# A seventh pass of the sequence DFT as seven block products, with two block sums made by accumulating DMAs

## The chip, the cores and the metric

The kernel runs on one core of a Trainium2 chip. The metric is the device time of one launch in microseconds (us); lower is better. A difference of 0.2% (1.4 us) is about what the measurement of this kernel can tell from no change.

## The reference

The reference is one block of an FNet: a Fourier mixing layer and then a gated feed-forward layer, both on a pre-normalized input with a residual. S = 2048 rows, D = 448 columns, Df = 1792.

```python
def _A_ref(x, dft_seq_re, dft_seq_im, dft_hid_re, dft_hid_im):
    a = jnp.einsum("bsd,ed->bse", x, dft_hid_re)
    b = jnp.einsum("bsd,ed->bse", x, dft_hid_im)
    y = jnp.einsum("ts,bse->bte", dft_seq_re, a) - jnp.einsum("ts,bse->bte", dft_seq_im, b)
    return y
def _B_ref(x, w_gate, w_up, w_down):
    g = jnp.einsum("bsd,df->bsf", x, w_gate)
    u = jnp.einsum("bsd,df->bsf", x, w_up)
    h = _gelu(g) * u
    return jnp.einsum("bsf,fd->bsd", h, w_down)
x = A_x
h = x + _A_ref(_layernorm(x), A_dft_seq_re, A_dft_seq_im, A_dft_hid_re, A_dft_hid_im)
h2 = h + _B_ref(_layernorm(h), B_w_gate, B_w_up, B_w_down)
```

## The kernel before

The kernel computes in f32 accuracy with f16 operands: each f32 operand is split into a high f16 part (`hi_part`, L108, on ScalarE/ACT) and a low f16 remainder (`lo_part`, L112 and L114, on VectorE/DVE), and each product is three f16 matmuls (hi·hi, hi·lo, lo·hi). There are three stages on TensorE (PE):

1. The DFT along the sequence (L637 and L509). The matrix W comes from DRAM in pieces, one piece per step, and every four steps make one pass. There are `N_STEPS` = 64 steps: 16 for the first two output pairs, and then twelve passes of four steps.
2. The DFT along the hidden dimension (`hid_mm`, L719), which is laid between the passes: 21 matmuls `y` for each half of an output pair.
3. The feed-forward, with gate/up products (L1028) in three blocks of 14 rounds `t`, and the down products (L1232) beside the last two blocks.

The order of all work is written out by hand: the program is issued in one loop over the steps `n`, and the tables `DFT_F`, `JIT_F`, `early`, `after`, `turns` and `PREP_AT` say in which step or round a piece stands. Each engine runs its own instructions in that order. SyncE (SP) issues all DMAs of the kernel before, also in that order.

A pass is computed in one of two ways. A *direct* pass (steps below `FAST`) has 24 matmuls of 448 columns a step. A *fast* pass (steps from `FAST` = 40 on, which are the last six passes) takes each pair of input rows and output rows as a 2x2 block product with seven block products instead of eight (Strassen-Winograd): 2 x 7 products x 3 terms = 42 matmuls of 224 columns a step, into four PSUM banks `acc_f`. It needs four sums of W's blocks, named S1 to S4 (`fast_sums`, L460 to L462, DVE), besides the raw blocks, and four sums of the rows of x, named T1 to T4 (`t_load`, `t_norm`, `t_sums`, `t_hi`, `t_lo`), which are made once in earlier steps. At the end of a pass `fast_out` combines the seven results on DVE (L538) and splits them into `zs`, and `z_turn` transposes `zs` by four DMAs.

The W data of one step are called a *unit* here. Units are prepared two or more steps ahead (`fast_at`): `seq_load` (SP, into `wr`), `fast_sums` (DVE), `fast_raw` (ACT hi, DVE lo of three raw blocks), `fast_split` (ACT hi, DVE lo of the four sums). The tiles `wr` and `sums` share a ring of five slots (tag `wr`): a load into a slot waits on SP until the DVE work that reads the slot's former tile is done.

The gate/up weights come in 14 chunks `f`. For each, `Weights` loads the raw data (SP), makes sums (DVE), splits them (ACT and DVE), and stores the f16 result in DRAM for the later blocks. Nine chunks (`DFT_F`) are split beside the DFT, the other five (`JIT_F` = 4, 6, 8, 10, 12) in the first feed-forward block, in round `t` = f - 2. GpSimd (POOL) computes nothing in the DFT; in the feed-forward it forms sums of the down weights (`down_sums`) and products (L1122).

Of the kernel before, what the change touches and what calls it, by code (L numbers as in the profile page):

```python
# [9 lines left out]
F32 = mybir.dt.float32  # L10
AF = mybir.ActivationFunctionType
ALU = mybir.AluOpType

P = 128
# [12 lines left out]
D_SC = 64.0  # L27
# [5 lines left out]
def kernel(  # L33
# [73 lines left out]
    def hi_part(dst, src, scale=1.0):  # L107
        A.activation(dst, src, AF.Copy, scale=scale)  # L108

    def lo_part(dst, src, hi, scale=1.0):  # L110
        if isinstance(scale, float) and scale == 1.0:
            V.tensor_sub(dst, src, hi)  # L112
        else:
            V.scalar_tensor_tensor(dst, src, scale, hi, op0=ALU.mult, op1=ALU.subtract)  # L114
# [293 lines left out]
    def step_of(n):  # L408

        k, qq = divmod(n - NT, 4)  # L410
        return 2 + k // 2, k % 2, qq

    def seq_load(n):
        wr[n] = dft.tile([P, 8 * P], F32, tag="wr", bufs=5, name=f"wr{n}")
        if n < NT:
            nc.sync.dma_start(wr[n].rearrange("p (b t) -> p b t", b=4), w_seq[8 * (n % 2) + n // 2])
            return
        p, part, qq = step_of(n)
        for i in range(2):
            dst = wr[n][:, i * 4 * P : (i + 1) * 4 * P].rearrange("p (g t) -> p g t", g=2)  # L420
            nc.sync.dma_start(dst, w_seq[8 * p + 2 * qq + i][:, 2 * part : 2 * part + 2, :])
# [24 lines left out]
    fast_w, fast_s, fast_t, fast_acc, fast_e = {}, {}, {}, {}, {}  # L446

    def fast_views(n):
        raw = wr[n].rearrange("p (i b t) -> p i b t", i=2, b=4)
        s = fast_s[n].rearrange("p (s i t) -> p s i t", s=4, i=2)  # L450
        src = raw[:, :, 0:3].rearrange("p i b t -> p i (b t)")
        dst = fast_w[n][0][:, :, : 6 * P].rearrange("p l (i b) -> p l i b", i=2)
        return raw, s, src, dst

    def fast_sums(n):
        fast_s[n] = dft.tile([P, 8 * P], F32, tag="wr", bufs=5, name=f"sums{n}")
        fast_w[n] = [fast_tile(n, k, **place) for k, place in enumerate(fast_places(n))]
        raw, s, src, dst = fast_views(n)
        by_block = raw.rearrange("p i b t -> p b i t")
        V.tensor_add(s[:, 0:2], by_block[:, 1:3], by_block[:, 3:4].to_broadcast([P, 2, 2, P]))  # L460
        V.tensor_add(s[:, 2], s[:, 1], raw[:, :, 1])
        V.tensor_add(s[:, 3], raw[:, :, 0], s[:, 2])  # L462
# [7 lines left out]

    def fast_raw(n):

        raw, s, src, dst = fast_views(n)
        hi_part(dst[:, 0], src, D_SC)
        lo_part(dst[:, 1], src, dst[:, 0], D_SC)

    def fast_split(n):

        w = fast_w[n][1]
        for part in slice(0, 4 * P), slice(4 * P, 8 * P):  # L480
            hi_part(w[:, 0, part], fast_s[n][:, part], D_SC)
        lo_part(w[:, 1], fast_s[n], w[:, 0], D_SC)

    def fast_a(n, i, l, name):
        if name in FORMS:
            k = 2 * FORMS.index(name) + i
# [247 lines left out]


    gu, gw = {}, {}
    DFT_F = ((13, 16, 0), (11, 18, 1), (9, 20, 0), (7, 22, 1), (5, 25, 0), (3, 27, 1), (0, 29, 0), (1, 33, 0), (2, 37, 0))
    JIT_F = range(4, 13, 2)

    early, after = {}, {}  # L740

    def at(where, n, *what):
        where.setdefault(n, []).extend(what)
# [49 lines left out]
    for j, n in ((0, 17), (1, 20), (4, 24), (5, 28), (6, 31), (2, 35), (3, 38), (7, 41)):  # L793
# [42 lines left out]
    for n in range(N_STEPS):  # L836
# [89 lines left out]
        for half in range(2):  # L926
# [3 lines left out]
                    z_out(*key)  # L930
            for what in after.get((n, half), ()):
                what()
    gu[JIT_F[0]] = Weights(JIT_F[0], JIT_F[0] % 3)
    z_turn(NP - 1)
    down_sums(0)
    gu[JIT_F[1]] = Weights(JIT_F[1], JIT_F[1] % 3)
# [331 lines left out]
    for q, t0, step, when in ((2, 5, 3, AT_A), (3, 14, 6, AT_B)):  # L1268
# [22 lines left out]
    right.close()  # L1291
    ps_ff = {
        tag: ctx.enter_context(tc.tile_pool(name=f"ps_{tag}", bufs=1, space=bass.MemoryType.PSUM, reuse_waits="tile"))
        for tag in ("a3", "X", "Y", "Z", "a0", "a1", "a2")
    }
    ps_ff["tr"] = ps_tr

# [7 lines left out]
    cur.x1()  # L1305
    cur.z1()
    prev = None
    PREP_AT = {0: 0, 1: 1, 3: 2, 5: 3, 7: 4, 9: 5, 11: 6}
    for t in range(NF):
        w = gu.get(t + 2) if t + 2 in JIT_F else None  # L1310
        n = PREP_AT.get(t)
# [46 lines left out]
        if t == 0:  # L1358
            down_sums(1)
        if t == NF - 1:  # L1360
            dn_lo(0)
        cur.z1()
# [209 lines left out]
```

## Time and profile before

| | |
|---|---|
| median of 3 runs | 703.41 us (703.22 to 703.43) |
| the profiled execution | 703.2 us |
| its span, first to last instruction | 701.1 us |
| PE busy in the span | 696.3 us |
| DVE, ACT, POOL busy | 551.0, 400.0, 95.4 us |
| mean granted TensorE clock | 1.000 |

The profile is of one execution. Its busy times say how long an engine had an instruction in it; a busy PE is not PE at its peak, so the time of a group of matmuls is read from the chain of work that ended last, which gives when a run of matmuls began and how long it carried the chain. `PEld` is the load of the stationary operand, which overlaps with PE. `SPq` is SP's queue of DMA issues; "to landing" is the time from a DMA's issue to its data being there. DMA share is the mean busy share of the 16 DMA engines; it is a sum of packet times, and it can pass 100%.

### The profile page before, as it was taken

What the parts mean: (1) busy time and instruction counts of PE and PEld (TensorE: products, weight loads), DVE (VectorE), ACT (ScalarE), POOL (GpSimd) and SP (SyncE); (2) the same over time, 40 slices, a digit from 0 to 9 for tenths busy, and PEclk for the clock granted to TensorE, in tenths of its full rate; (3) what the DMA queues carried; (4) which work ended last, traced back from release to release, by engine and by line L of the source; (5) the groups of instructions that cost most, each with busy time, mean ns of one, the idle gap of its engine ahead of it and who ended that gap; (6) DMA issues with size and microseconds to landing.
All of it is one profiled execution on the core that took longest, in us unless ns stands there. A gap on an engine that the chain in (4) does not pass through costs nothing.

```text
span 701.1 us, 13638 instructions
## 1 busy us (share of the span) xinstructions
PE 696.3 (99%) x5164; PEld 500.6 (71%) x5164; DVE 551.0 (79%) x1187; ACT 400.0 (57%) x787; POOL 95.4 (14%) x88
## 2 busy tenths in 40 slices
PE   9999999999999999999999999999999999999998
PEld 5555555555557889997644444469999999999997
DVE  7998667786798999986547798767777867899786
ACT  5876556666676566564526666555555453655631
POOL 0000000000000000000223333311020111232224
PEclk9999999999999999999999999999999999999999
DMA  8798578999997487384836878797879985877612
GB/s 276 252 255 303 121 267 227 334 288 289 269 287 195 141 195 200 117 205 179 233 125 212 288 242 236 189 326 231 245 209 326 247 299 170 318 274 276 239 39 79
DMA packets 116321, 161.29 MB, mean 230 GB/s; under 512 B 61984, under 2 KB 80544, under 8 KB 116256
## 3 DMA queue, kind: packets, MB, share of 16 engines
q1 hardware_dynamic: 116256, 160.43, 76.0%
q8 instruction: 40, 0.66, 0.4%
q14 instruction: 25, 0.20, 0.1%
HBM read 112.16 MB, written 34.34 MB: 209 GB/s over the span
## 4 chain that ended last, share of the span: by engine, by line
PE 98%; issue 1%; DMA 0%; DVE 0%; ACT 0%
PE acc L637 26%; PE acc_d L1232 15%; PE pY L1028 15%; PE acc_f L509 14%; PE pZ L1028 10%; PE pX L1028 10%; PE y L719 9%; DMA x<-in_x_dram 0%; ACT dn_w L108 0%; ACT v L958 0%; DVE st_x L122 0%; DVE xs L149 0%; DVE hr L1508 0%; ACT sd_x L129 0%; DVE r_x L373 0%
## 5 line engine op out<-in xcount | busy, mean ns | idle before, releaser
L637 PE MATMUL acc<-xs,ws 128*128 128x448 f16 x960 | 183.1, 352 | 0.1
L1028 PEld LDWEIGHTS <-gw 128*128 128x128 f16 x1443 | 140.9, 98 | 51.6
L637 PEld LDWEIGHTS <-ws 128*128 128x128 f16 x960 | 93.9, 98 | 87.7 <-DVE ws L114 0.2
L1232 PE MATMUL acc_d<-wd,dn_w 128*128 128x224 f16 x1008 | 110.6, 259 | 0.0
L1232 PEld LDWEIGHTS <-dn_w 128*128 128x128 f16 x1008 | 97.0, 98 | 1.9
L1028 PE MATMUL pY<-hops,gw 128*128 128x256 f16 (+1 forms) x629 | 98.1, 298 | 0.0
L509 PEld LDWEIGHTS <-ws 128*128 128x128 f16 x1008 | 96.6, 98 | 1.3
L1122 POOL TENSOR_TENSOR hs<-hs,c 128x256 f32<-128x256 f32 (+1 forms) x42 | 59.5, 1417 | 247.6 <-ACT c L1120 185.3
L114 DVE SCALAR_TENSOR_TENSOR ws<-wr,ws 128x1024 f16<-128x1024 f32 (+2 forms) x66 | 72.0, 1092 | 20.8 <-ACT ws L108 16.3
L108 ACT ACTIVATE ws<-wr 128x1024 f16<-128x1024 f32 (+2 forms) x66 | 61.9, 941 | 13.4 <-DMA wr<-in_w_seq_dram 8.0
L509 PE MATMUL acc_f<-t,ws 128*128 128x224 f16 x576 | 68.2, 259 | 0.0
L1028 PE MATMUL pZ<-hops,gw 128*128 128x256 f16 (+1 forms) x407 | 67.1, 298 | 0.0
L1028 PE MATMUL pX<-hops,gw 128*128 128x256 f16 (+1 forms) x407 | 67.1, 298 | 0.0
L719 PE MATMUL y<-wh,z 128*128 128x448 f16 x336 | 66.2, 352 | 0.0
L1073 ACT ACTIVATE pY<-pX 128x256 f32<-128x256 f32 (+1 forms) x42 | 18.4, 439 | 66.3 <-PE pX L1028 63.0
L215 POOL TENSOR_TENSOR wd_s<-wd 128x448 f32<-128x448 f32 x7 | 9.7, 1390 | 337.1 <-DVE e L538 336.3
L509 PE MATMUL acc_f<-xs,ws 128*128 128x224 f16 x432 | 55.1, 259 | 0.0
L719 PEld LDWEIGHTS <-z 128*128 128x128 f16 x336 | 32.9, 98 | 29.7
L1038 DVE SCALAR_TENSOR_TENSOR c<-pZ,u 128x256 f32<-128x256 f32 (+1 forms) x42 | 21.4, 510 | 38.8 <-PE pZ L1028 22.8
L1084 ACT ACTIVATE u<-pY 128x256 f32<-128x256 f32 (+1 forms) x42 | 19.1, 454 | 53.5 <-PE pY L1028 53.4
L112 DVE TENSOR_TENSOR dn_w<-dn_s,dn_w 128x640 f16<-128x640 f32 x48 | 41.5, 865 | 1.5 <-ACT dn_w L108 1.4
L108 ACT ACTIVATE dn_w<-dn_s 128x640 f16<-128x640 f32 x48 | 34.9, 728 | 12.1 <-DVE dn_s L1194 12.0
(144 smaller groups left out, 909.5 us busy)
## 6 DMA issues: line engine op xcount, KB each, us to landing
gw<-w_dram SPq DMA_DIRECT2D x37, 896.0 KB, 6.5
wr<-in_w_seq_dram SPq DMA_DIRECT2D x100, 256.0 KB, 4.6
hid_dram<-hs SPq DMA_DIRECT2D x27, 512.0 KB, 5.9
hid<-hid_dram SPq DMA_DIRECT2D x54, 256.0 KB, 5.8
w_dram<-gu_w SPq DMA_DIRECT2D x14, 896.0 KB, 6.5
gu_raw<-in_w_gu_dram SPq DMA_DIRECT2D x28, 384.0 KB, 6.1
wr<-in_w_seq_dram SPq DMA_DIRECT2D x14, 512.0 KB, 5.2
x<-in_x_dram SPq DMA_DIRECT2D x16, 224.0 KB, 3.1
```

Source lines behind the costliest of these rows:

```text
L108: A.activation(dst, src, AF.Copy, scale=scale)
L112: V.tensor_sub(dst, src, hi)
L114: V.scalar_tensor_tensor(dst, src, scale, hi, op0=ALU.mult, op1=ALU.subtract)
L509: PE.matmul(fast_sum(n, k), fast_a(n, i, lw, a), fast_b(j, lx, b), start=j == 0 and m == 0 and k % 2 == 0, stop=j == NT // 2 - 1 and m == ...
L637: PE.matmul(acc[key][:, :D], w[:, lw, block * P : (block + 1) * P], xs[c][:, lx, :], start=c == 0 and m == 0, stop=c == NT - 1 and m == 2,)
L719: PE.matmul(y[:, :D], z[p][:, lz, k, g * P : (g + 1) * P], wh[:, lw, k, :], start=p == NP - 1 and k == 0 and m == 0, stop=k == 6 and m == ...
L1028: PE.matmul(ps, w[:, wl, wa + ws, :], ops[:, m + ms, :], start=first and n == 0, stop=last and n == len(terms) - 1, skip_group_check=True,)
L1038: V.scalar_tensor_tensor(dst, ps, SC, other, op0=ALU.mult, op1=ALU.add)
L1073: A.activation(self.Y, self.X, AF.Copy)
L1084: A.activation(self.u2, self.Y, AF.Copy, scale=SC)
L1122: G.tensor_mul(c22, c22, self.cols(self.c12))
L1232: PE.matmul(ps, w[:, la, a, :], wd[n][:, lb, b, :], start=n == 0 and m == 0 and opens, stop=n == NC - 1 and m == 2, skip_group_check=True,)
```

## The change

It moves `FAST` from step 40 to step 36, so that one more pass of four steps (steps 36 to 39) is computed as seven block products.

In a fast unit, the sums S1 and S3 are no longer made by DVE. SP loads two blocks (256 columns for each of the two output rows) straight into the sums' tile, and two DMAs issued by POOL then add the fourth block, read once for each of the two, onto them (`accum_op=add`). The fourth block is no longer loaded into `wr`, which so holds three blocks. One tile of the ring now holds such sums of two units (`pair`); S2 and S4 are made by DVE into a tile `more` of another ring (tag `xt`). The low parts of the sums come in two instructions of 512 columns instead of one of 1024.

Since the fast units begin four steps earlier, the other work of the DFT is packed into fewer steps: the chunks of `DFT_F` are eight instead of nine, and the sums T1 to T4 are made in steps 17 to 37 instead of 17 to 41. Chunk 2 becomes the first of `JIT_F`: its raw data are loaded at step `N_STEPS` - 6 and split in round 0 of the feed-forward, and so the splits of the down weights (`PREP_AT`) move to later rounds. The list of the feed-forward's PSUM pools is rotated by two, so that the names stand for the same banks relative to the last pass.

```diff
     def seq_load(n):
+        if n >= FAST:
+            fast_load(n)
+            return
...
-    FAST = N_STEPS - 24
+    FAST = N_STEPS - 28
...
+    def fast_load(n):
+        p, part, qq = step_of(n)
+        wr[n] = dft.tile([P, 2, 3 * P], F32, tag="wr", bufs=5, name=f"wr{n}")
+        if n % 2 == 0:
+            pair["now"] = dft.tile([P, 2, 2, 2, P], F32, tag="wr", bufs=5, name=f"sums{n}")
+        fast_s[n] = pair["now"][:, n % 2]
+        blocks = [w_seq[8 * p + 2 * qq + i].rearrange("p g t -> p (g t)")[:, 4 * part * P :] for i in range(2)]
+        for i in range(2):
+            nc.sync.dma_start(fast_s[n][:, i], blocks[i][:, P : 3 * P].rearrange("p (s t) -> p s t", s=2))
+        for i in range(2):
+            nc.sync.dma_start(wr[n][:, i], blocks[i][:, 0 : 3 * P])
+        for i in range(2):
+            G.dma_start(
+                fast_s[n][:, i],
+                blocks[i][:, None, 3 * P : 4 * P].to_broadcast([P, 2, P]),
+                accum_op=ALU.add,
+            )
...
     def fast_sums(n):
-        fast_s[n] = dft.tile([P, 8 * P], F32, tag="wr", bufs=5, name=f"sums{n}")
         fast_w[n] = [fast_tile(n, k, **place) for k, place in enumerate(fast_places(n))]
-        raw, s, src, dst = fast_views(n)
-        by_block = raw.rearrange("p i b t -> p b i t")
-        V.tensor_add(s[:, 0:2], by_block[:, 1:3], by_block[:, 3:4].to_broadcast([P, 2, 2, P]))
-        V.tensor_add(s[:, 2], s[:, 1], raw[:, :, 1])
-        V.tensor_add(s[:, 3], raw[:, :, 0], s[:, 2])
+        t = dft.tile([P, 2, 2, P], F32, tag="xt", bufs=3, name=f"more{n}")
+        raw, sa = fast_views(n)[0], fast_s[n]
+        fast_s[n] = sa, t
+        V.tensor_add(t[:, :, 0], sa[:, :, 1], raw[:, :, 1])
+        V.tensor_add(t[:, :, 1], raw[:, :, 0], t[:, :, 0])
...
     def fast_split(n):
-        w = fast_w[n][1]
-        for part in slice(0, 4 * P), slice(4 * P, 8 * P):
-            hi_part(w[:, 0, part], fast_s[n][:, part], D_SC)
-        lo_part(w[:, 1], fast_s[n], w[:, 0], D_SC)
+        w = fast_w[n][1].rearrange("p l (h i s t) -> p l h i s t", h=2, i=2, s=2)
+        for h in range(2):
+            hi_part(w[:, 0, h], fast_s[n][h], D_SC)
+        for h in range(2):
+            lo_part(w[:, 1, h], fast_s[n][h], w[:, 0, h], D_SC)
...
-    JIT_F = range(4, 13, 2)
+    JIT_F = range(2, 13, 2)
...
-    for f, n in ((0, N_STEPS - 7), (2, N_STEPS - 4), (1, N_STEPS - 3)):
+    for f, n in ((0, N_STEPS - 7), (1, N_STEPS - 3)):
...
+    at(after, (N_STEPS - 6, 0), lambda: gu.update({JIT_F[0]: Weights(JIT_F[0], JIT_F[0] % 3)}))
...
-    PREP_AT = {0: 0, 1: 1, 3: 2, 5: 3, 7: 4, 9: 5, 11: 6}
+    PREP_AT = {1: 0, 3: 1, 5: 2, 7: 3, 9: 4, 11: 5, 12: 6}
```

Three places show what moves. The first is DVE's work on one unit (`ws_0` takes the raw blocks, `ws_1` the sums). Before:

```order
L460 TENSOR_TENSOR sums_2338<-wr_2173 128x512
L461 TENSOR_TENSOR sums_2338<-sums_2338,wr_2173 128x256
L462 TENSOR_TENSOR sums_2338<-wr_2173,sums_2338 128x256
L114 SCALAR_TENSOR_TENSOR ws_0_2339<-wr_2173,ws_0_2339 128x768
L114 SCALAR_TENSOR_TENSOR ws_1_2340<-sums_2338,ws_1_2340 128x1024
```

Now, with `sums` filled by DMAs alone:

```order
L480 TENSOR_TENSOR more_2363<-sums_2174,wr_2173 128x2x128
L481 TENSOR_TENSOR more_2363<-wr_2173,more_2363 128x2x128
L114 SCALAR_TENSOR_TENSOR ws_0_2361<-wr_2173,ws_0_2361 128x768
L114 SCALAR_TENSOR_TENSOR ws_1_2362<-sums_2174,ws_1_2362 128x512
L114 SCALAR_TENSOR_TENSOR ws_1_2362<-more_2363,ws_1_2362 128x512
```

The add of 512 columns is gone, and DVE's first add of a unit now reads what the DMAs summed.

The second place is SP's queue about the second fast pass (`tx` are rows of x for the T sums, `hx` rows for the residual, `z` the transposes after a pass). Before:

```order
L421 DMA wr_2272<-in_w_seq_dram 128x512 x2
L421 DMA wr_2349<-in_w_seq_dram 128x512 x2
L733 DMA h_dram_140<-hx_1_1978 128x896
L563 DMA tx_0_2385<-in_x_dram 128x448
L563 DMA tx_1_2386<-in_x_dram 128x448
L693 DMA hx_0_2401<-in_x_dram 128x2x448
L351 DMA w_dram_147<-gu_w_2275 128x3584
L658 DMA_TRANSPOSE z_2425<-zs_2130 128x7x128 x4
L421 DMA wr_2462<-in_w_seq_dram 128x512 x2
```

Now:

```order
L459 DMA sums_2174<-in_w_seq_dram 128x256 x2
L461 DMA wr_2301<-in_w_seq_dram 128x384 x2
L459 DMA sums_2373<-in_w_seq_dram 128x256 x2
L461 DMA wr_2372<-in_w_seq_dram 128x384 x2
L754 DMA h_dram_140<-hx_1_2027 128x896
L459 DMA sums_2373<-in_w_seq_dram 128x256 x2
L461 DMA wr_2487<-in_w_seq_dram 128x384 x2
L459 DMA sums_2536<-in_w_seq_dram 128x256 x2
L461 DMA wr_2535<-in_w_seq_dram 128x384 x2
L714 DMA hx_0_2551<-in_x_dram 128x2x448
L679 DMA_TRANSPOSE z_2574<-zs_2193 128x7x128 x4
```

Each unit has four loads where it had two, the sums' pair ahead of the raw blocks, and one tile `sums` is named by two units.

The third place is POOL's queue between its constants at the start and its first work for the feed-forward. Before:

```order
L93 MEMSET sign_t 64x1
L94 MEMSET sign_t 64x1
L215 TENSOR_TENSOR wd_s_4064<-wd_0_3967 128x448
L217 TENSOR_TENSOR wd_s_4064<-wd_0_3967 128x448
L218 TENSOR_TENSOR wd_s_4064<-wd_0_3967 128x224
```

Now, the first five of them:

```order
L94 MEMSET sign_t 64x1
L463 DMA sums_1921<-in_w_seq_dram 128x2x128 x4
L463 DMA sums_2008<-in_w_seq_dram 128x2x128 x4
L463 DMA sums_2174<-in_w_seq_dram 128x2x128 x4
L463 DMA sums_2373<-in_w_seq_dram 128x2x128 x4
```

Fourteen such groups of four, 56 accumulating DMAs in all, now stand ahead of POOL's first `down_sums`.

More of the change, by code (lines that the diff above doesn't have):

```diff
@@ L445 @@
     PRODUCTS = ("A11", "B11"), ("A12", "B21"), ("S2", "T2"), ("S3", "T3"), ("S1", "T1"), ("S4", "B22"), ("A22", "T4")
-    fast_w, fast_s, fast_t, fast_acc, fast_e = {}, {}, {}, {}, {}
+    fast_w, fast_s, fast_t, fast_acc, fast_e, pair = {}, {}, {}, {}, {}, {}
+    def fast_load(n):
[15 more added lines that the diff above has]
+            )
     def fast_views(n):
-        raw = wr[n].rearrange("p (i b t) -> p i b t", i=2, b=4)
-        s = fast_s[n].rearrange("p (s i t) -> p s i t", s=4, i=2)
-        src = raw[:, :, 0:3].rearrange("p i b t -> p i (b t)")
+        src = wr[n]
+        raw = src.rearrange("p i (b t) -> p i b t", b=3)
         dst = fast_w[n][0][:, :, : 6 * P].rearrange("p l (i b) -> p l i b", i=2)
-        return raw, s, src, dst
+        return raw, src, dst
     def fast_sums(n):
-        fast_s[n] = dft.tile([P, 8 * P], F32, tag="wr", bufs=5, name=f"sums{n}")
         fast_w[n] = [fast_tile(n, k, **place) for k, place in enumerate(fast_places(n))]
-        raw, s, src, dst = fast_views(n)
-        by_block = raw.rearrange("p i b t -> p b i t")
-        V.tensor_add(s[:, 0:2], by_block[:, 1:3], by_block[:, 3:4].to_broadcast([P, 2, 2, P]))
-        V.tensor_add(s[:, 2], s[:, 1], raw[:, :, 1])
-        V.tensor_add(s[:, 3], raw[:, :, 0], s[:, 2])
+        t = dft.tile([P, 2, 2, P], F32, tag="xt", bufs=3, name=f"more{n}")
[3 more added lines that the diff above has]
+        V.tensor_add(t[:, :, 1], raw[:, :, 0], t[:, :, 0])
     def fast_tile(n, k, pool=None, **place):
@@ L471, in fast_raw @@
     def fast_raw(n):
-        raw, s, src, dst = fast_views(n)
+        raw, src, dst = fast_views(n)
         hi_part(dst[:, 0], src, D_SC)
@@ L477, in fast_split @@
     def fast_split(n):
-        w = fast_w[n][1]
-        for part in slice(0, 4 * P), slice(4 * P, 8 * P):
-            hi_part(w[:, 0, part], fast_s[n][:, part], D_SC)
-        lo_part(w[:, 1], fast_s[n], w[:, 0], D_SC)
+        w = fast_w[n][1].rearrange("p l (h i s t) -> p l h i s t", h=2, i=2, s=2)
[3 more added lines that the diff above has]
+            lo_part(w[:, 1, h], fast_s[n][h], w[:, 0, h], D_SC)
     def fast_a(n, i, l, name):
         if name in FORMS:
-            k = 2 * FORMS.index(name) + i
+            f = FORMS.index(name)
+            k = f // 2 * 4 + 2 * i + f % 2
             return fast_w[n][1][:, l, k * P : (k + 1) * P]
@@ L736 @@
     gu, gw = {}, {}
-    DFT_F = ((13, 16, 0), (11, 18, 1), (9, 20, 0), (7, 22, 1), (5, 25, 0), (3, 27, 1), (0, 29, 0), (1, 33, 0), (2, 37, 0))
-    JIT_F = range(4, 13, 2)
+    DFT_F = ((13, 14, 0), (11, 16, 1), (9, 18, 0), (7, 20, 1), (5, 22, 0), (3, 24, 1), (0, 28, 0), (1, 32, 0))
+    JIT_F = range(2, 13, 2)
     early, after = {}, {}
@@ L792 @@
     at(after, (N_STEPS - 2, 0), lambda: down_load(0), lambda: down_load(1))
-    for j, n in ((0, 17), (1, 20), (4, 24), (5, 28), (6, 31), (2, 35), (3, 38), (7, 41)):
+    for j, n in ((0, 17), (1, 20), (4, 23), (5, 26), (6, 29), (2, 31), (3, 34), (7, 37)):
         at(after, (n - 2, 1), lambda j=j: t_load(j))
@@ L932 @@
                 what()
-    gu[JIT_F[0]] = Weights(JIT_F[0], JIT_F[0] % 3)
     z_turn(NP - 1)
@@ L1293 @@
         tag: ctx.enter_context(tc.tile_pool(name=f"ps_{tag}", bufs=1, space=bass.MemoryType.PSUM, reuse_waits="tile"))
-        for tag in ("a3", "X", "Y", "Z", "a0", "a1", "a2")
+        for tag in ("Y", "Z", "a0", "a1", "a2", "a3", "X")
     }
@@ L1357 @@
             down_sums(PREP_AT[t + 1])
-        if t == 0:
-            down_sums(1)
         if t == NF - 1:
```

## The prediction

> **What bounds the kernel now.** I read the page first, then PE's waits, then the chain in order of time, then stages.
>
> ```profile
> span 701.1 us, 13638 instructions
> PE 696.3 (99%) x5164; PEld 500.6 (71%) x5164; DVE 551.0 (79%) x1187; ACT 400.0 (57%) x787; POOL 95.4 (14%) x88
> PE 98%; issue 1%; DMA 0%; DVE 0%; ACT 0%
> ```
>
> ```profile
> PE pw L102 <- POOL sign_t L93: 1.4, 1, 1.4
> PE acc_d L1232 <- ACT v L958: 0.2, 1, 0.2
> ```
>
> The chain is PE nearly everywhere, and PE waits only 0.2 us after its start. So each microsecond of PE work removed is gained if nobody is late. The chain gives the price of a pass of either kind (start, us carried, what):
>
> ```profile
> 107.04 18.16 PE acc L637 x96
> ...
> 261.56 16.10 PE acc_f L509 x168
> 277.66 3.97 PE y L719 x21
> 281.63 16.10 PE acc_f L509 x168
> ```
>
> A direct pass carries the chain for 18.16 us (96 matmuls), a fast one for 16.10 us (168), twice the same. Fast pass and `y` together make a period of 20.07 us. What stops more passes from being fast is seen in the stages (us, then busy times of PE, PEld, DVE, ACT, POOL, clock, DMA share, GB/s):
>
> ```profile
> 160.00:200.00 40.00, 40.00 (x214) 20.70 (x212) 29.55 (x60) 25.75 (x49) 0.00 (x0) 1.00 1.09 268
> 237.00:257.00 20.00, 20.00 (x191) 18.08 (x189) 19.61 (x36) 12.88 (x25) 0.00 (x0) 1.00 0.63 137
> 257.00:277.00 20.00, 20.00 (x191) 18.08 (x189) 19.50 (x38) 11.36 (x22) 0.00 (x0) 1.00 0.82 209
> 277.00:297.00 20.00, 20.00 (x191) 18.08 (x190) 18.59 (x31) 11.18 (x21) 0.00 (x0) 1.00 0.36 120
> 297.00:317.00 20.00, 20.00 (x191) 18.08 (x189) 17.61 (x30) 10.92 (x21) 0.00 (x0) 1.00 0.82 215
> 340.00:360.00 20.00, 20.00 (x98) 9.35 (x97) 11.72 (x17) 10.00 (x16) 6.52 (x7) 1.00 0.73 205
> 360.00:400.00 40.00, 40.00 (x190) 18.38 (x188) 26.35 (x47) 23.07 (x40) 11.90 (x10) 1.00 0.56 191
> ```
>
> In the fast passes DVE is busy 19.61 of 20 us, though PE never waits. ACT has a third free, POOL is idle, and the DMA engines are far from the 1.09 that the direct stage (first row) stands without a PE wait.
>
> **The change, part by part.** *PE.* One pass goes from 18.16 to 16.10 us: -2.06 us. The other PE work is the same.
>
> *DVE and ACT.* A unit's rows:
>
> ```profile
> L460 DVE TENSOR_TENSOR sums<-wr 128x512 f32<-128x512 f32 x24 | 16.4, 685 | 0.9 <-DMA wr<-in_w_seq_dram 0.9
> L461 DVE TENSOR_TENSOR sums<-sums,wr 128x256 f32<-128x256 f32 x24 | 10.2, 425 | 0.8
> L462 DVE TENSOR_TENSOR sums<-wr,sums 128x256 f32<-128x256 f32 x24 | 10.2, 425 | 0.8
> L114 DVE SCALAR_TENSOR_TENSOR ws<-wr,ws 128x768 f16<-128x768 f32 x24 | 22.9, 952 | 1.4 <-ACT ws L108 1.4
> L114 DVE SCALAR_TENSOR_TENSOR ws<-sums,ws 128x1024 f16<-128x1024 f32 x24 | 29.2, 1218 | 0.2
> L114 DVE SCALAR_TENSOR_TENSOR ws<-wr,ws 128x512 f16<-128x512 f32 x4 | 2.7, 686 | 0.0
> L114 DVE SCALAR_TENSOR_TENSOR ws<-wr,ws 128x1024 f16<-128x1024 f32 x38 | 46.5, 1223 | 19.4 <-ACT ws L108 14.9 <-DMA wr<-in_w_seq_dram 2.4 <-DMA hx<-in_x_dram 1.7
> ```
>
> Before: 685 + 425 + 425 + 952 + 1218 = 3.71 us. Now: 425 + 425 + 952 + 2 x 686 = 3.17 us, so 0.53 us less per unit and 2.1 us less per period: 19.6 becomes 17.5 of 20. The four new fast units cost DVE 4 x (3.17 - 1.22) = 7.8 us more than direct ones, about the step-32 stage, where it is busy 29.55 of 40. ACT keeps its instructions and its free third. Both cost PE nothing; if DVE's reserve (2.5 us a period) were eaten by waits for the sums, `fast_out` would come late and PE would next wait for a bank of `acc_f`.
>
> *SP.* A unit has four loads instead of two, and 28 units come of 24:
>
> ```profile
> L421 SPq DMA_DIRECT2D wr<-in_w_seq_dram x96: 322/431/1587, 50.3 to 312.7; - x96
> L658 SPq DMA_TRANSPOSE z<-zs x32: 1220/1296/2272, 76.4 to 344.8; - x32
> ```
>
> That is 2 x 0.43 us more a unit; 16 x 0.43 + 4 x 1.30 = 12.1 us of a 20 us period, so SP is not full. The loads are moved past nothing but each other; each even unit's waits for its slot, and the transposes and the `hx` load behind wait with it, as they did behind `wr`.
>
> *The sums' way (new).* SP loads two blocks, POOL waits for them, writes two DMAs, and these land; only then may DVE's first add run. Neither a POOL DMA nor an accumulating one is in this trace, so I bound them:
>
> ```profile
> wr<-in_w_seq_dram SPq DMA_DIRECT2D x8, 256.0 KB, 2.8
> ```
>
> ```profile
> wr<-in_w_seq_dram SPq DMA_DIRECT2D x6, 256.0 KB, 4.4
> ```
>
> ```profile
> L1122 POOL TENSOR_TENSOR hs<-hs,c 128x256 f32<-128x256 f32 (+1 forms) x42 | 59.5, 1417 | 247.6 <-ACT c L1120 185.3
> L1122 POOL TENSOR_TENSOR hs<-hs,c x42: 727/1268/4880, 348.1 to 667.5; 128x256 f32<-128x256 f32 x28, 128x512 f32<-128x512 f32 x14
> ```
>
> The two `wr` rows are median landings in 277 to 297 us and in 217 to 237 us. Issue of two loads 0.86 us; landing 2.8 to 4.4, I take 3.6; POOL's two DMAs between SP's 0.43 and POOL's mean 1.42 each, I take the latter (POOL is the same engine), 2.8; landing of the accumulation between 2.8 and twice 4.4 (its target is read too), I take 4.4. Sum 11.7 us, bounds 7.3 and 16.9.
>
> How much is allowed follows from the ring. Tiles are taken in the order `wr` 36, `sums` 36, `wr` 37, `wr` 38, `sums` 38, so an even unit k gets the slot of `wr` k-3 and its load starts when DVE has split that unit's raw blocks. From there to its own raw split are the sums' way and 0.85 + 0.95 = 1.80 us; one whole unit (3.17) later the load of unit k+4 may start. So four units take at least the sums' way + 4.97 us; PE takes 20.07 for them. The sums' way may last 15.1 us, and I expect 3.4 us to spare. I cost it at nothing.
>
> The POOL rows also warn: its instruction lasts 0.73 to 4.88 us, that is, it is held at times, by as much as 4.2 us. The Trainium skill ("SBUF — State Buffer", Who interferes with whom) explains such holds by a port pair that POOL shares with DVE: a DVE instruction in a two-port mode keeps POOL from writing DMA descriptors, while one with two SBUF inputs blocks only POOL's reads. DVE's rows here mostly have two inputs, so by the second clause the sum stays; by the first, that of rival A, it would not.
>
> *DMA engines.* Packets of the loads alone, and of loads with transposes:
>
> ```profile
> q1 hardware_dynamic: 1283, 2.35, 35.1%
> ```
>
> ```profile
> DMA packets 4363, 2.74 MB, mean 137 GB/s; under 512 B 3439, under 2 KB 3439, under 8 KB 4361
> q1 hardware_dynamic: 4361, 2.71, 62.8%
> ```
>
> In 277 to 297 us, 35.1% of 16 x 20 us over 1283 packets is 87.5 ns each, 47.8 ns per KB. In 237 to 257 us the 3439 short packets take (201.0 - 922 x 87.5 ns) = 120.3 us, 35 ns each. A unit of 512 KB was 1.57 us of all 16 engines; now 640 KB by plain loads is 1.96 us, and 512 packets of 512 B accumulate. These cost 24 ns at the rate per KB, or 175 ns if each were two full packets; I take 35, the nearest size: 1.12 us a unit. A period had a mean share of 0.66, 13.2 us, of it 6.3 for units; now 6.9 + 4 x (1.96 + 1.12) = 19.2 of 20 us, 96%. That is under the 1.09 of the direct stage, so I cost it at nothing. By bounds it is 89% to 186%; the 1.09 is passed at 55 ns a packet.
>
> *Chunk 2 in the feed-forward.* Round 0 now has a chunk and round 1 a split of down weights, the mix that 360 to 400 us already has at 26.35 of 40 us of DVE, where PE does not wait. Nothing, at most 0.5 us. Its store moves too, and the reload of 896 KB at step 60 is gone.
>
> Sum: -2.06 + 0. The profiled execution of 703.2 (2.1 us around its span) would be 701.1; the median of the runs stood 0.2 above it, so 701.4.
>
> **The rivals.** *A, slower: POOL is held by DVE while it writes the accumulating DMAs.* For it: DVE is busy nearly all the time there, and the 4.88 us. Against: the minimum of 0.73, and a slack of 3.4 us. It decides from a sums' way of 15.4 us on (15.1 + 2.06 / 7), since each microsecond over 15.1 costs 7 us (28 units / 4). At the upper bound of 16.9 us: +13, 714. With both DMAs held for 4.88 us the way is 0.86 + 4.4 + 9.8 + 8.8 = 23.9 us: +61, 762. The skill's box on DVE blocking such DMAs (the same page) is this case.
>
> *B, slower: the DMA engines become the bound.* Decides beyond 55 ns an accumulating packet. At 70 ns (two reads of 35) a period needs 14.7 + 4 x 2.24 = 23.7 us of packet time, at 1.09 that is 21.7, 1.7 over, x 7: +12, 713. For it: each packet reads two places. Against: 268 GB/s and more were carried before.
>
> *C, no change that can be told.* At the entry, unit 36's loads stand on SP behind the `hops` transposes of step 30 and are wanted at step 32, some 7 us later, against a way of 11.7: DVE waits 5 us. Its reserve there (26%) and the four steps until PE uses the unit should cover it; if a bank is released late, PE pays 0.7 to 3 us, and 702.1 to 704.4 comes out.
>
> **How the numbers follow.** The forecast, with its own range of 700.8 to 702.0: 0.57. C: 0.16. A: 0.13. B: 0.14. A measurement tells 0.2%, 1.4 us: below 702.0 is faster, above 704.8 slower. So faster 0.57, same 0.16, slower 0.27. The range takes the forecast, C, and the nearest third of A and B, which leaves out 0.18 above: 700.8 to 709.
>
> **What would show it.** Right: `acc` has 864 matmuls, `acc_f` 1176, PE's waits stay near 1.6 us, and 36 to 63 run at 20.07 us per four steps and a `y`. DVE's first add of a unit (L480) waits for `sums` only about step 32; DVE near 17.5 of 20 us. DMA share 0.9 to 1.1 in the fast passes. A shows as L480 waiting for `sums` in every even unit with the DMA share low; B as the same with a share at 1.1 and all landings longer; C as one PE wait about the first fast pass. A wrong price of POOL's DMAs or of the accumulating packets would make the prediction wrong.

## The result, and the profile after

The changed kernel takes 727.17 us (median of five runs, 726.5 to 729.04) against 703.41 (703.2 to 703.53): a ratio of 1.0345, 95% interval 1.0329 to 1.0361. It is slower, where 701.4 us was forecast. The profiled execution took 726.94 us.

The page of the changed kernel: span, PE's line, the chain's shares, and the three groups of DFT matmuls.

```profile
span 725.2 us, 14049 instructions
PE 705.7 (97%) x5236; PEld 511.4 (71%) x5236; DVE 546.0 (75%) x1210; ACT 403.4 (56%) x796; POOL 164.0 (23%) x144
PE 50%; issue 2%; DMA 1%; ACT 1%; DVE 0%; POOL 0%; POOLq 0%; DVEq 0%
L658 PE MATMUL acc<-xs,ws 128*128 128x448 f16 x864 | 164.8, 353 | 0.0
L530 PE MATMUL acc_f<-t,ws 128*128 128x224 f16 x672 | 84.9, 268 | 9.2 <-DVE e L559 5.6
L530 PE MATMUL acc_f<-xs,ws 128*128 128x224 f16 x504 | 68.1, 268 | 2.9 <-DVE ws L114 2.9
```

The work is what was announced: 864 direct matmuls and 672 + 504 = 1176 fast ones. But the chain, which was PE for 98% of the span before, is PE for 50% now. PE is busy 705.7 us, where the same matmuls take 694.2 in a kernel without the accumulating DMAs (below), and it now waits. Its waits from 150 to 370 us (total, times, longest):

```profile
PE acc_f L530 <- DVE e L559: 5.6, 2, 3.0
PE acc_f L530 <- DVE ws L114: 5.0, 5, 2.6
PE y L740 <- ACT y L721: 2.3, 1, 2.3
PE acc_f L530 <- ACT t L108: 1.0, 1, 1.0
PE acc_f L530 <- DVE t L112: 0.4, 1, 0.4
```

They add up to 14.3 us, and 705.7 - 694.2 = 11.5 us are slower matmuls. Together that is 25.8 us, all of the difference between 725.2 and the 699.4 us of that kernel's span. Stages show where the slower matmuls are (busy times as before, then the granted clock and the DMA share):

```profile
240.00:260.00 20.00, 16.36 (x118) 12.61 (x116) 11.26 (x28) 9.14 (x17) 10.56 (x10) 0.83 0.91 187
260.00:280.00 20.00, 20.00 (x191) 18.08 (x190) 16.55 (x34) 12.90 (x27) 8.96 (x8) 1.00 1.12 217
280.00:300.00 20.00, 17.33 (x154) 14.20 (x151) 9.20 (x22) 6.25 (x11) 7.35 (x6) 0.99 1.18 221
300.00:320.00 20.00, 18.91 (x156) 16.39 (x156) 18.73 (x38) 12.87 (x25) 9.79 (x8) 0.83 0.91 200
```

DVE, which was busy 17.6 to 19.6 us of 20 before, has 9 to 19: it is no bound, it starves. The two stretches with a clock of 0.83 lie at and behind pauses of PE. The timelines of SP, POOL, DVE and PE (start, us; in brackets the idle time before and its releaser) show one such pause from its beginning, and the two later holds of SP (L559 is `fast_out`, which reads `acc_f` and so frees its bank):

```profile
224.99 11.87 SPq L679 DMA_TRANSPOSE z<-zs  x4
236.91 1.05 SPq L459 DMA_DIRECT2D sums<-in_w_seq_dram  x2
...
239.99 2.44 POOL L463 DMA_DIRECT2D sums<-in_w_seq_dram  x2 [11.20 <-DMA sums<-in_w_seq_dram]
...
248.56 0.42 DVE L480 TENSOR_TENSOR more<-sums,wr 128x256 f32<-128x256 f32 x1 [8.52 <-DMA sums<-in_w_seq_dram]
...
250.83 0.38 DVE L559 SCALAR_TENSOR_TENSOR e<-acc_f,e 128x224 f32<-128x224 f32 x1
...
251.26 0.73 PE L530 MATMUL acc_f<-t,ws 128*128 128x224 f16 x6 [3.02 <-DVE e L559]
...
274.34 9.69 SPq L679 DMA_TRANSPOSE z<-zs  x4
...
323.03 8.40 SPq L679 DMA_TRANSPOSE z<-zs  x4
```

SP issues the four transposes of a `z` and is held by them for 11.87 us. Only then does it issue the next unit's loads; these land, POOL issues its two DMAs, they land, and 23.6 us after the hold began DVE adds, having waited 8.5 us. `fast_out` stands behind that add in DVE's order, and PE, which waits for its bank, starts again after 3.02 us. Before, the same three places in SP's queue read:

```profile
221.15 7.51 SPq L658 DMA_TRANSPOSE z<-zs  x4
...
261.62 5.25 SPq L658 DMA_TRANSPOSE z<-zs  x4
...
303.20 7.17 SPq L658 DMA_TRANSPOSE z<-zs  x4
```

The landings from 180 to 360 us (queue: packets, MB, share of 16 engines; then issues, KB each, median us to landing) show the changed kernel's:

```profile
q0 software_dynamic: 15024, 7.24, 37.4%
wr<-in_w_seq_dram SPq DMA_DIRECT2D x52, 192.0 KB, 4.5
sums<-in_w_seq_dram POOLq DMA_DIRECT2D x54, 128.0 KB, 6.1
sums<-in_w_seq_dram SPq DMA_DIRECT2D x50, 128.0 KB, 4.1
z<-zs SPq DMA_TRANSPOSE x16, 7.2
```

Without the accumulating DMAs SP's three rows land in 3.6, 3.5 and 3.8 us: everything is slower here. An accumulating packet took 37.4% x 16 x 180 us / 15024 = 72 ns.

### The profile page after: what moved, and what is told of

Same layout as the page of the kernel before. It is cut to its first block, busy times and chain, and to the rows that moved or that the text cites. A ratio compares the mean times of both kernels' runs of the same rounds, so it can differ in the third digit from the quotient of the medians.

```text
span 725.2 us, 14049 instructions
## 1 busy us (share of the span) xinstructions
PE 705.7 (97%) x5236; PEld 511.4 (71%) x5236; DVE 546.0 (75%) x1210; ACT 403.4 (56%) x796; POOL 164.0 (23%) x144
## 4 chain that ended last, share of the span: by engine, by line
PE 50%; issue 2%; DMA 1%; ACT 1%; DVE 0%; POOL 0%; POOLq 0%; DVEq 0%
PE acc_d L1253 15%; PE pY L1049 14%; PE pX L1049 9%; PE pZ L1049 9%; PE y L740 2%; PE acc_f L530 1%; DMA sums<-in_w_seq_dram 1%; ACT dn_w L108 0%; ACT v L979 0%; ACT y L731 0%; POOL sums L463 0%; ACT hx L729 0%; ACT y L721 0%; DVE more L481 0%; DVE more L480 0%
## 5 line engine op out<-in xcount | busy, mean ns | idle before, releaser
L1049 PEld LDWEIGHTS <-gw 128*128 128x128 f16 x1404 | 136.9, 98 | 47.2
L658 PE MATMUL acc<-xs,ws 128*128 128x448 f16 x864 | 164.8, 353 | 0.0
L658 PEld LDWEIGHTS <-ws 128*128 128x128 f16 x864 | 84.5, 98 | 79.0 <-issue 0.2
L463 POOL DMA_DIRECT2D sums<-in_w_seq_dram x56 | 68.5, 1461 | 276.2 <-DMA wr<-in_w_seq_dram 178.0
L530 PEld LDWEIGHTS <-ws 128*128 128x128 f16 x1176 | 116.0, 101 | 19.5 <-issue 7.6
L1049 PE MATMUL pY<-hops,gw 128*128 128x256 f16 (+1 forms) x612 | 94.2, 296 | 0.0
L530 PE MATMUL acc_f<-t,ws 128*128 128x224 f16 x672 | 84.9, 268 | 9.2 <-DVE e L559 5.6
L114 DVE SCALAR_TENSOR_TENSOR ws<-wr,ws 128x1024 f16<-128x1024 f32 (+2 forms) x66 | 70.9, 1076 | 14.9 <-ACT ws L108 14.6
L530 PE MATMUL acc_f<-xs,ws 128*128 128x224 f16 x504 | 68.1, 268 | 2.9 <-DVE ws L114 2.9
L1049 PE MATMUL pZ<-hops,gw 128*128 128x256 f16 (+1 forms) x396 | 64.4, 296 | 0.0
L1049 PE MATMUL pX<-hops,gw 128*128 128x256 f16 (+1 forms) x396 | 64.4, 296 | 0.0
L1049 PEld LDWEIGHTS <-gu_w 128*128 128x128 f16 x234 | 22.9, 98 | 27.6
```

Of the source, the lines that this page charges most:

```text
L463: G.dma_start(fast_s[n][:, i], blocks[i][:, None, 3 * P : 4 * P].to_broadcast([P, 2, P]), accum_op=ALU.add,)
L530: PE.matmul(fast_sum(n, k), fast_a(n, i, lw, a), fast_b(j, lx, b), start=j == 0 and m == 0 and k % 2 == 0, stop=j == NT // 2 - 1 and m == ...
L658: PE.matmul(acc[key][:, :D], w[:, lw, block * P : (block + 1) * P], xs[c][:, lx, :], start=c == 0 and m == 0, stop=c == NT - 1 and m == 2,)
L1049: PE.matmul(ps, w[:, wl, wa + ws, :], ops[:, m + ms, :], start=first and n == 0, stop=last and n == len(terms) - 1, skip_group_check=True,)
```

## The experiments

Two theories stood at first: B, the accumulating packets overfill the DMA engines; and L, the way from the issue of the loads to the finished sums is too long because two landings follow one another. L' adds to it that SP is held in front of that way. Times are medians; each ratio is against the kernel before in the same series.

**Without the accumulating DMAs** (`no_acc`).

```diff
-        for i in range(2):
-            G.dma_start(
...
-                accum_op=ALU.add,
-            )
```

> The changed kernel without its accumulating DMAs (it leaves out adding the fourth block to S1 and S3; SP's plain loads of both remain). Theory B (the accumulating packets overfill the DMA engines): the share of the DMA engines in the seven fast passes falls from 1.2 to about 0.75, DVE stops waiting for the sums, PE's clock is 1.00 and the time is 700.5 to 702.5, what the prediction gave. Theory L (the way is too long because two landings follow one another, whatever the engines carry): the same time, since the second landing is gone as well. Rival R (the rest of the change costs it: the seventh pass's work on DVE, the moved weight chunk, the order of the PSUM pools): 710 or more, with PE waits that remain.

701.08 us, ratio 0.9964 (0.9951 to 0.9977). All the loss is gone, with the seventh pass, the moved chunk and SP's four loads in place. Rival R falls; B and L both stand. PE's busy time is 694.2 us, its clock 1.00. SP's transposes of `z` from 200 to 345 us (min/median/max ns), first of this kernel, then of the changed one:

```profile
L673 SPq DMA_TRANSPOSE z<-zs x16: 1227/1253/2366, 220.3 to 344.2; - x16
```

```profile
L679 SPq DMA_TRANSPOSE z<-zs x12: 1673/2254/4033, 225.0 to 329.8; - x12
```

**The same sums on DVE, and on GpSimd** (`seven_dve`, `seven_pool`): seven passes and the moved chunk, with loads and sums of the kernel before, in the second with one engine changed.

```diff
-        V.tensor_add(s[:, 0:2], by_block[:, 1:3], by_block[:, 3:4].to_broadcast([P, 2, 2, P]))
+        G.tensor_add(s[:, 0:2], by_block[:, 1:3], by_block[:, 3:4].to_broadcast([P, 2, 2, P]))
```

> The same with that add on DVE, as in the kernel before: seven passes alone, without accumulating DMAs. DVE is then at 19.6 of 20 us in the fast passes, and the four new units bring 4 x (3.71 - 1.22) = 10.0 us to the 29.6 of 40 about step 32. Theory: it just holds, and the time is 701.4 to 702.5. Rival: DVE is over there and PE waits for it: 703 to 708.

> Seven fast passes and the moved weight chunk as in the changed kernel, but the loads of the kernel before (two of 256 KB a unit) and the add of S1 and S3 as one 128x512 instruction on GpSimd. If the seven passes and the chunk cost nothing by themselves: 701.4 (700.8 to 702.0), with DVE at 19.6 - 4 x 0.69 = 16.9 of 20 us in the fast passes. Rival: GpSimd is held while DVE works, the add takes 4.9 us in place of 1.4, DVE's next adds come late and PE waits at banks: 703 to 712.

On DVE 701.09 us, ratio 0.9964 (0.9951 to 0.9978); on GpSimd 701.48, ratio 0.9971 (0.9960 to 0.9982). Both beat both kernels. With the add on DVE, a fast stage reads:

```profile
240.00:260.00 20.00, 20.00 (x191) 18.08 (x190) 19.61 (x36) 13.10 (x26) 0.00 (x0) 1.00 0.67 155
```

DVE is at 19.61 of 20 us and PE is full: the 0.4 us left were enough, and taking the add away from DVE was worth nothing. On GpSimd DVE did not get freer either: 19.64 of 20 in the same kind of stage, not the 16.9 expected. Its own rows grew: from 215 to 330 us the add of L462 took 839 ns where it took 425, and the low part of 1024 columns 1331 ns where it took 1218.

**Six passes with accumulating DMAs** (`six_acc`): the kernel before with `fast_load`, `fast_sums`, `fast_split` of the changed one, `FAST = N_STEPS - 24`.

> The kernel before (six fast passes, no chunk moved) with the accumulating DMAs for its 24 units. If they cost what they cost in seven passes, in proportion: 703.6 + 24 / 28 x 26.1 = 726. Rival: most of the loss comes of their meeting the seventh pass's entry and the transfers of the direct stage: 708 to 716.

728.92 us (721.94 to 731.08), ratio 1.0345 (1.0291 to 1.0399). The loss belongs to the DMAs, not to the seventh pass.

**Plain copies in their place, and these alone** (`pool_plain`, `pool_only`). The first drops one line, the second also SP's loads of the sums:

```diff
-                accum_op=ALU.add,
...
-        for i in range(2):
-            nc.sync.dma_start(fast_s[n][:, i], blocks[i][:, P : 3 * P].rearrange("p (s t) -> p s t", s=2))
```

> The changed kernel with its two GpSimd DMAs a unit as plain copies (they overwrite S1 and S3 with the fourth block; the addition is left out). Size, packets, issuing engine and order (after the plain loads have landed) are as in the changed kernel. Theory B by reading and writing the target: a packet falls from about 72 ns to 35 ns or less, the DMA share to about 1.0, DVE's waits for the sums shrink and the time is 701 to 704. Theory L (two landings one after the other, and GpSimd's issue of 1.2 to 1.4 us each): the way stays near what it is, DVE still waits and the time is 720 to 727. In between (way shorter by 1 to 2 us at 7 us of time each): 710 to 720.

> The run with plain copies, now without SyncE's loads of the sums as well: GpSimd's two plain copies are all that fills S1 and S3 (the other block and the addition are left out). One landing instead of two in a row, GpSimd's issue and engine as in the run with plain copies (715.4). Theory L (what the plain copies cost is the second landing behind the first, with SyncE late): 701 to 703. Rival (GpSimd's queue itself is slow to start or to land, or the traffic decides): 708 to 715.

715.39 us (712.78 to 718.33), ratio 1.0168 (1.0141 to 1.0196): more than half of the loss is there without any accumulation. Its rows:

```profile
q0 software_dynamic: 2586, 7.06, 14.5%
sums<-in_w_seq_dram POOLq DMA_DIRECT2D x53, 128.0 KB, 4.6
```

The same bytes went in 2586 packets and took 14.5% of the engines instead of 37.4%. And with one landing, 701.50 us, ratio 0.9970 (0.9958 to 0.9982): GpSimd's queue as such costs nothing. So it matters how the sums are filled. This run takes away the second landing and SP's part in it together, and so cannot tell the row of two landings from SP being late with the first.

**One accumulating DMA a unit, and 1 KB packets** (`acc_half`, `acc_1kb`).

```diff
-        for i in range(2):
+        for i in range(1):
             G.dma_start(
```

```diff
-                blocks[i][:, None, 3 * P : 4 * P].to_broadcast([P, 2, P]),
+                blocks[i][:, 2 * P : 4 * P].rearrange("p (s t) -> p s t", s=2),
```

> The changed kernel with one accumulating DMA a unit in place of two (it leaves out adding the fourth block of the second row of blocks). The two add 4 x 2.44 us of 16 engines to a period (72 ns a packet), so half takes the period from some 24.5 to 19.6 us of packet time. Theory B (the engines' load decides): DMA share about 1.0, short waits, 701 to 706. Theory L (the two landings in a row decide, with whatever else makes a unit's loads late): the way is shorter only by one issue of 1.2 us and some landing time, as in the run with plain copies, and the time is 712 to 720.

> The changed kernel with accumulating DMAs that read 256 columns in a row in place of the fourth block twice (S1 and S3 get the third and fourth block added, so the sums are others): as many bytes, half as many packets if a packet then has 1 KB. If the price is by the packet: GpSimd's issue falls from 1.2 to about 0.7 us, the DMA share as in the run with half the accumulations, 702 to 715. If it is by the byte: packets of about 140 ns, and 722 to 728.

Half the accumulations: 706.05 us, ratio 1.0041 (1.0026 to 1.0056), close to theory B's 701 to 706, so for the moment B stood again. Longer packets: 720.71 (718.32 to 726.21), ratio 1.0257 (1.0210 to 1.0304). The queue's row there, over 180 to 360 us:

```profile
q0 software_dynamic: 7852, 7.14, 29.3%
```

That is 107 ns for a packet of 909 bytes: nearly half the packets, about a fifth less engine time, so the price is neither by the packet nor by the byte alone, and the time lies between the two ranges that were expected. Two of GpSimd's issues fell from 2.44 to 1.75 us. The median fell by 6.5 us, but the profiled execution, at 726.21 us, did not; which of the two lower prices the median owes it to is not shown.

**Accumulation with one landing** (`acc_zero`): GpSimd zeroes the tile instead of SP loading it.

```diff
-        for i in range(2):
-            nc.sync.dma_start(fast_s[n][:, i], blocks[i][:, P : 3 * P].rearrange("p (s t) -> p s t", s=2))
+        G.memset(fast_s[n], 0.0)
```

> The changed kernel with the tile set to zero by GpSimd in place of SyncE's loads of the sums, and the two accumulating DMAs behind that (the sums then hold only the fourth block). One landing in place of two, but the accumulating packets are all there: a period's packet time falls by the 4 x 0.78 us of the plain loads alone. Theory B (72 ns a packet decides wherever it stands): 712 to 722. Theory L (only the row of two landings decides): 701 to 705.

703.73 us (702.61 to 709.43), ratio 1.0010 (0.9990 to 1.0029). Its stages and the queue:

```profile
220.00:240.00 20.00, 20.00 (x190) 17.92 (x188) 16.03 (x40) 10.99 (x19) 11.37 (x11) 1.00 1.19 204
...
260.00:280.00 20.00, 20.00 (x191) 18.09 (x189) 13.93 (x31) 11.11 (x22) 11.01 (x12) 1.00 1.28 232
```

```profile
q0 software_dynamic: 13838, 6.67, 32.3%
```

All accumulating packets are there, at 67 ns each, none of them behind a load of SP, and the engines' share stands at 1.19 and 1.28, over any stage shown of the changed kernel, while PE is full. Theory B as a bound is refuted: full engines do not stop PE here. Landings and SP's transposes are longer beside them, and it then matters what stands behind these.

**SP's hold** (`z_act`, `z_spread`, `z_twice`, `z_none`). Four ways to change how long the transposes of a `z` hold SP in front of the sums' loads: issue them from ScalarE; issue them two and two; issue each twice (in the kernel without accumulating DMAs); leave out those of passes 3 to 6.

```diff
# z_act
-                nc.sync.dma_start_transpose(z[p][:, l, :, g * P : (g + 1) * P], zs[p][:, g, l, :])
+                nc.scalar.dma_start_transpose(z[p][:, l, :, g * P : (g + 1) * P], zs[p][:, g, l, :])
# z_spread (z_turn takes the list of g)
-        at(after, (n, half), lambda p=p: z_turn(p))
+        at(after, (n, half), lambda p=p: z_turn(p, (0,) if p > 2 else (0, 1)))
+        if p > 2:
+            at(after, (n + 2, half), lambda p=p: z_turn(p, (1,)))
# z_twice, in z_turn
-            for l in range(2):
+            for l in (0, 1, 0, 1) if p > 2 else (0, 1):
# z_none, in z_turn
+        if 3 <= p <= 6:
+            z[p] = z[2]
+            return
```

> The changed kernel with the transposes of z issued by ScalarE in place of SyncE. In the changed kernel each of these holds SyncE for 2.24 us (1.31 before), four in a row for 9.7 us, and the loads of the next units stand behind them. Theory L': this hold is what makes the sums late, and without it the time falls to 706 to 716. Theory B alone: the engines carry as much as before, and it stays at 722 to 728. It may also rise over 728 if ScalarE's own work comes late behind the transposes.

> The changed kernel with the four transposes of a z issued two and two, the second pair two steps later; same transfers. SyncE is then held for some 4.8 us at a time in place of 9.7, and the unit behind gets its loads that much earlier. If this hold is a part of the way (L'): 712 to 721. If only the engines' load counts (B): 724 to 729.

> The kernel without the accumulating DMAs (701.1), with each transpose of a z issued twice (to the same place, from the fourth z on): SyncE is then held for some 10 us at a time, as in the changed kernel, but the sums have one landing. Theory: hold and way add up. Hold 10 and way 4.4 make 15, less than the 18 of the run with plain copies that lost 14 us, so little is lost: 701 to 704. Rival: the hold alone is what costs, whatever the way: 712 to 725.

> The changed kernel, accumulating DMAs and both landings as they are, without the transposes of the z of passes 3 to 6 (their y is made from the z before, so it leaves these four transposes' data out). SyncE is then held by no transpose of z while fast units are loaded. Theory (hold and way add up, and about 15 to 17 us of them are free; changed kernel 9.7 + 14 = 23.7, run with transposes twice 14.5 + 4.4 = 19): here 0 + 13 to 14, so 700.5 to 705. If the two landings by themselves are too long for the ring: 712 to 722. If the accumulating packets fill the engines: their share falls only by the transposes' packets (7.5 us of all engines per z), and the time stays over 708.

From ScalarE: 756.72 us, ratio 1.0743 (1.0716 to 1.0770). This told nothing about SP, because ScalarE was now held itself:

```profile
ACT ws L108 <- issue: 35.3, 3, 16.4
```

Two and two: 719.47, ratio 1.0217 (1.0196 to 1.0239), 7.7 us off with the same transfers. Twice each: 719.65 (718.55 to 723.48), ratio 1.0235 (1.0206 to 1.0265), although no sum has a second landing. This missed my 701 to 704 and lies in the range of the rival, that the hold alone costs. The hold was not 10 us but this, and it contains waits for the first copies (SP waited 10.1 us for `z`, in nine pieces, from 180 to 360 us):

```profile
225.83 13.80 SPq L673 DMA_TRANSPOSE z<-zs  x8
...
270.28 15.21 SPq L673 DMA_TRANSPOSE z<-zs  x8
```

Without those transposes, both landings and all accumulating DMAs kept: 702.58 us (701.31 to 704.72), ratio 0.9987 (0.9977 to 0.9997).

```profile
220.00:240.00 20.00, 20.00 (x191) 18.08 (x189) 16.67 (x41) 10.86 (x19) 9.76 (x8) 1.00 1.03 216
240.00:260.00 20.00, 20.00 (x191) 18.08 (x189) 19.21 (x41) 14.57 (x29) 7.86 (x7) 1.00 0.97 200
```

```profile
sums<-in_w_seq_dram POOLq DMA_DIRECT2D x53, 128.0 KB, 5.9
sums<-in_w_seq_dram SPq DMA_DIRECT2D x50, 128.0 KB, 4.4
```

The two landings are as long as in the changed kernel, and PE is full. So the way alone fits the ring; hold and way together do not. The run takes the packets of those transposes away as well; that it is not the lower load rests on the run with the tile zeroed, where PE was full at 1.19 and 1.28. The direct trial, all transposes kept but issued behind the next unit's loads, was not made. Put side by side, each from its profiled execution (mean hold of the three `z` between 215 and 335 us, and way = issue 0.9 + SP's landing + GpSimd's issues + their landing, medians):

| kernel | hold, us | way, us | sum | its time over 701.1 us |
|---|---|---|---|---|
| no accumulating DMAs | 5.7 | 0.9 + 3.5 = 4.4 | 10.1 | 0.2 |
| no transposes of z 3 to 6 | 0 | 0.9 + 4.4 + 2.4 + 5.9 = 13.6 | 13.6 | 1.3 |
| tile zeroed (raw loads stand behind the hold) | 8.4 | 0.9 + 4.7 = 5.6 | 14.0 | 2.7 |
| one accumulating DMA | 7.4 | 0.9 + 3.7 + 1.2 + 5.1 = 10.9 | 18.3 | 4.5 |
| transposes twice | 14.6 | 4.4 | 19.0 | 19.2 |
| plain copies | 8.6 | 0.9 + 3.9 + 1.4 + 4.6 = 10.8 | 19.4 | 11.7 |
| six passes, accumulating | 9.0 | 0.9 + 4.1 + 2.4 + 6.2 = 13.6 | 22.6 | 18.3 (over 703.6) |
| changed kernel | 10.0 | 0.9 + 4.1 + 2.4 + 6.1 = 13.5 | 23.5 | 25.8 |
| 1 KB packets | 11.2 | 0.9 + 4.2 + 1.8 + 5.6 = 12.5 | 23.7 | 25.1 |

Up to 14 us of hold and way cost under 3 us, from 18 us on 4.5 to 25.8. The engines' mean share from 200 to 345 us orders the rows worse: at 1.00 (tile zeroed) 2.7 us were lost, at 0.85 (transposes twice) 19.2 and at 0.89 (plain copies) 11.7. The order of the rows at 18 to 19 us is not explained by the sum, nor is the run with the transposes two and two (4.1 and 13.4 us, yet 18 over): it has twice as many holds. So the sum tells the kernels that lose from those that do not; how much is lost it gives only roughly.

**Work on DVE alone** (`dve_more`, `dve_lump`): the kernel before, with the add of S2 done more often, spread over all units or in one unit of four. No DMA is touched.

```diff
+        for _ in range(3):                          # dve_more
+        for _ in range(9 if n % 4 == 2 else 1):     # dve_lump
             V.tensor_add(s[:, 2], s[:, 1], raw[:, :, 1])
```

> The kernel before, with DVE's add of S2 (425 ns) done three times over in each of the 24 units: 0.85 us a unit more, 3.4 a period, of which DVE has 0.4 to 2.4 free. No DMA is changed. PE should wait some 8 to 14 us in all. If TensorE's granted clock falls only when the DMA engines are overfull, it stays 1.00 here and the time is 703.6 plus PE's waits, 712 to 718. If a PE that pauses is itself granted less afterwards, as the windows of the changed kernel suggest (0.83 to 0.93 behind each pause), the time is up by twice the waits, 720 to 730.

> The kernel before with the same extra work on DVE as the run before it of this kind (8 more adds of S2 per period, 3.4 us), but all in one unit of four, so that PE's pauses are fewer and longer; no DMA is changed. In all runs so far the granted clock stood at 1.00 where PE's longest wait was 1.8 us or less, and fell to 0.83 to 0.97 where one was 2.5 us or more. Theory: the length of a pause decides. If a pause here exceeds 2.5 us, a window shows a clock under 0.95 and the time is some 2 to 5 us over the run with spread work (713.8); if DVE's lead takes up the lump (longest wait under 2 us), the clock stays 1.00 and the time is 710 to 714. Rival: the clock falls only beside overfull DMA engines, and it is 1.00 here with pauses over 2.5 us too.

Spread: 713.83 us, ratio 1.0145 (1.0130 to 1.0160), mean clock 1.000, as was expected if only overfull DMA engines lower the clock. In one unit: 718.78, ratio 1.0211 (1.0194 to 1.0229), mean clock 0.995, which is against that. PE's waits of the first, then of the second with a stage and the `y` behind its pause of 2.8 us:

```profile
PE acc_f L511 <- DVE ws L114: 6.6, 12, 1.8
```

```profile
PE acc_f L510 <- DVE ws L114: 8.0, 7, 3.1
PE y L720 <- ACT y L701: 2.8, 1, 2.8
```

```profile
240.00:260.00 20.00, 16.86 (x148) 14.57 (x147) 19.40 (x39) 10.28 (x22) 0.00 (x0) 0.91 0.38 99
```

```profile
342.37 5.82 PE L720 MATMUL y<-wh,z 128*128 128x448 f16 x21 [2.82 <-ACT y L701]
```

The same 21 matmuls carried the chain for 3.97 us before. With the DMA engines at 0.38, the clock fell behind pauses of 2.8 and 3.1 us, and not behind one of 1.8. So the lower clock comes of PE's pauses, not of full DMA engines. In the changed kernel a pause of 2.3 us had the same slow `y` behind it:

```profile
349.73 5.82 PE L740 MATMUL y<-wh,z 128*128 128x448 f16 x21 [2.33 <-ACT y L721]
```

In all traces of this case, from 20 us on, pauses of 0.9 to 1.83 us have a clock of 1.00 behind them (but for one that follows right on a longer one), and those of 2.46 us or more a lower one (0.57 to 0.82 over the next 8 us). Of four pauses of 2.31 to 2.33 us two lowered it and two did not, one of the latter beside a DMA share of 1.11 (`six_acc`, at 283.71 us). The Trainium skill ("TensorE: Matmul & The Clock Gate", Why this matters for your kernels) warns of gaps over some 3 us, after which the clock is halved until PE has been busy for a while. The traces agree in kind (the granted clock is 0.50 from 252 to 258 us of the changed kernel); here gaps of 2.3 us could already do it.

## Why the prediction was wrong, by its own steps

**PE, -2.06 us: right.** PE's busy time went from 696.3 to 694.3 us in the kernel with seven passes and sums on DVE, and the median from 703.7 to 701.1.

**DVE: right, and beside the point.** Relieving it was costed at nothing and was worth nothing: 19.61 of 20 us hold without a PE wait in the seven passes too. The path that it named for a DVE that must wait for the sums, `fast_out` late and PE at a bank of `acc_f`, is the one in the trace (5.6 us of PE's waits).

**SP: the step that failed.** It was weighed by its busy time, 12.1 of 20 us, with 4 x 1.30 us for the transposes of a `z`. It should have been read as a queue. The step says that transposes wait behind a load; it left out that the next unit's loads wait behind the transposes. These were also 1.7 times as long (median 2254 ns), so the hold was 8.4 to 11.9 us. It belongs in front of the sums' way, and 15.1 us allowed against 10.0 + 13.5 us would have shown the loss. Even the prediction's own figures, 4 x 1.30 + 11.7 = 16.9 us, pass 15.1.

**The sums' way: 11.7 us taken, 13.5 measured,** inside the bounds of 7.3 to 16.9. The two landings were 4.1 and 6.1 where 3.6 and 4.4 were taken; GpSimd's issues 2.4 where 2.8 was taken. The allowance of 15.1 us fits as far as the runs go: a way of 13.6 us without a hold costs 1.5 us.

**DMA engines: price wrong, and their limit too.** A packet was taken at 35 ns and took 72, beyond the 55 ns from which rival B was to decide. But B's mechanism is not what happened: a share of 1.28 was carried with PE full, so 1.09 was no limit, only a share that the trace of before happened to show. What is longer beside the full engines are the landings and SP's transposes of `z`: medians of 1.6 to 2.5 us in the runs with a mean share of 0.89 or more from 200 to 345 us (the run without those transposes apart), against 1.25 to 1.37 in those with 0.60 to 0.85. Why a transpose holds SP longer there was not tried.

**Price of an excess.** 7 us for each microsecond over, from 28 units in fours, does not describe it: the loss comes in three groups of waits of 2.3 to 3.7 us, one behind each `z` from 225 us on, 4.7 us of waits before them (215 to 236 us), and 11.5 us of slow matmuls, for which the prediction had no term.

**Rival A** is excluded: GpSimd's accumulating DMAs took 1.2 to 2.4 us each with DVE at work beside them, never 4.88. The Trainium skill's case of a GpSimd DMA held by DVE ("SBUF — State Buffer", Who interferes with whom) is not this one; its clause on DVE instructions with two inputs, by which the sum stayed, agrees. **Rival C** was there at most as a part: of the 4.7 us of waits between 215 and 236 us, 1.4 come late in the first fast pass and for the T sums, and 3.3 in the second, for low parts of units. Ahead of them SP issued two `hops` transposes in 4.97 us (4.80 without the accumulating DMAs) and the `z` of 183 us in 8.10 (5.52 without); which of these made the waits was not tried. **Chunk 2 in the feed-forward** cost nothing that can be told: kernels that have it reach 701.1 us.

## What to carry to other kernels

A queue is not judged by its busy share. Walk it in order: whatever is issued ahead of a load on the same queue is part of that load's latency, with the length it will have beside the new traffic; add that hold to the whole way from issue to first use, every landing of it, before comparing with what the buffers allow. And a pause of TensorE can cost more than its length from some 2.3 us on, so one long lateness is dearer than the same lateness in small pieces (718.8 against 713.8 us for the same extra work on DVE).

## What the runs showed that was not expected

- An accumulating packet of some 480 bytes takes 67 to 72 ns, so 128 KB take 272 packets and about 19 us of engine time; as plain copies from the same queue, 128 KB took some 49 packets and 7.9 us (14.5% x 16 x 180 us over 53 DMAs).
- GpSimd issues a DMA in 0.72 us plain and, accumulating, two in 2.44 us.
- The share of the DMA engines can stand at 1.28 for 20 us with TensorE full.
- Moving the transposes to ScalarE cost 29.6 us more than the change itself: a queue that also computes must not be held by transposes.
